# RWKV-6 and a SiLU layer on one core: the first two units loaded in runs of 16 tokens, and the way of their bonus sums

## Chip, core and metric

The kernel runs on one core of one Trainium2 chip. TensorE (PE, with weight loads PEld) multiplies matrices, VectorE (DVE), ScalarE (ACT) and GpSimd (POOL) work element by element, SyncE (SP) issues most DMAs; ACT issues some as well. Each engine does its instructions in order and waits on semaphores. The metric is the device time of one execution in microseconds (us).

## What is computed

The reference is a linear attention with decay and a bonus `u`, then two matrix products with SiLU between them:

```python
for t in range(S):                       # B, H, S, D = 4, 8, 768, 48
    cur = einsum('bhd,bhe->bhde', u[None] * k[t], v[t])
    y[t] = einsum('bhd,bhde->bhe', r[t], state + cur)
    state = w[t][:, :, :, None] * state + einsum('bhd,bhe->bhde', k[t], v[t])
x = y.transpose(0, 2, 1, 3).reshape(3072, 384)
h = x @ w_in                             # 384 x 2048
out = (h / (1 + exp(-h))) @ w_out        # 2048 x 384
```

The bonus of one token is the sum over d of r*u*k: it is the diagonal of the matrix of scores of a head. All is float32.

## The kernel before

The sequence is cut into 6 blocks of L = 128 tokens, the batch into 2 pairs; that gives 12 units of 128 tokens by NB = 2 batch rows by 8 heads. Within a unit the state is not stepped: queries and keys grow by the decay over 7 levels (NL) of blocks of 1, 2, 4 to 64 tokens, and at each level TensorE makes the scores between neighbouring blocks. The output of a unit then passes through both matrix products. The order of work is written out by hand (lines 1384 to 1463): every engine gets its instructions in the order of these calls, and while a unit's levels run, the matrix products of earlier units and the rounding of weights are put between them.

The change touches the first two units (i < NTOK = 2), which have a way of their own to load tokens.

- `load_tokens` (114) with `load_twos` (108) brings k, r and w of a unit to `raw`, two neighbouring tokens of one head in a run: 192 KB a DMA, one DMA for each batch row, a partition holding a pair of tokens of all 8 heads. For unit 0 the second batch row is issued by ACT, all else by SP.
- `turn_in` (370) turns such a tile on TensorE, channels to partitions, by matmuls with the identity as the moving operand, 128 columns each; `s` says whether the even or the odd tokens. `turn_out` (381) copies the PSUM bank to `tk`, `tr` or `tw` on ACT; for k the second batch row is written backwards.
- `bonus` (426) multiplies: step 0 r of odd by k of even tokens (needed for level 0), step 1 r by k, step 2 by `u_bc`, which holds u for all heads in each partition (line 281, 192 KB by a DMA broadcast). `bonus_sum` (446) adds over d on DVE into `own_sums`.
- `bonus_spread` (577) brings these sums to the layout of the scores, on TensorE with the matrix `spread` of zeros and ones that `make_spread` (302) builds; `bonus_write` (598), for unit 0 in four parts by `bonus_part` (606), puts them into `score` on DVE with a mask (line 602).
- `odd_ones` (658, ACT), `start_keys` (663), `grow_queries` (625), `product` (408) are level 0: they multiply keys (L670), queries (L628) and decays (L414). `odd_keys` (613, ACT), `grow_keys` (631, POOL, L646) and `scores` (725: TensorE L712 or L704, then `keep_masked` on DVE, L722) are the later levels.
- `beat` (1374) transposes the identity on TensorE, n times; the result is used by nobody.
- `head_weight` (ACT, 221), `tail_weight` (ACT, 232), `join_weight` (DVE, L247, L248) and `add_weight` (POOL, L260) round one piece of the weights; `up` (1079) is the first matrix product, `x_products` (883) the output of the attention. `tail_weight` writes to the PSUM tile `p_w`, in which unit 0's spread sums lie before it.

PSUM banks are given out in turn: `bank("p_m")` and `bank("p_sc")` alternate between two banks each. The first two units' steps are in this order (lines 1384 to 1387):

```python
do((make_spread,), (beat, 16), *both(turn, 0, "k"), (odd_ones, 0), (bonus, 0, 0), (bonus, 0, 1), *both(turn, 0, "r"),
   (bonus_sum, 0, 0), (clear_state,), (clear_rest,), *back(turn, 0, "w"), (bonus, 0, 2), (bonus_sum, 0, 1), (start_keys, 0, nc.vector, True),
```

then levels 1 to 6 of unit 0 (1393) with unit 1's turns between them, then unit 1 (1396 on). `kernel.py` in the profile has these line numbers.

## Time and profile before

| | us |
|---|---|
| median of 3 runs | 566.67 (566.48 to 567.2) |
| the profiled execution | 567.41 |
| its span | 565.6 |

| engine | busy us | share of the span |
|---|---|---|
| PE | 555.8 | 98% |
| DVE | 477.0 | 84% |
| POOL | 395.7 | 70% |
| ACT | 274.5 | 49% |

The granted clock of TensorE is 1.0 over the whole span, DMA moved 57.59 MB in 206485 packets. The span is counted from the first instruction. A timeline line gives start, duration, engine, source line, operation, what is written and read, shapes and count; in brackets stands how long the engine was idle before it and what ended that. A line of the chain gives start, duration and what worked. A "q" behind an engine is its sequencer, which waits and issues and does not compute. fp32 matmuls are recorded twice each, so 8 matmuls show as 16.

### The profile page before, as it was taken

The page shows a single profiled execution, that of the slowest core. Times are in us where ns is not written, and L with a number is a line of the kernel's source. Part 1 is how long each engine was busy: PE and PEld are TensorE (multiplying, and loading weights), DVE is VectorE, ACT ScalarE, POOL GpSimd, SP SyncE. Part 2 cuts the span into 40 slices and gives each one's busy share as a digit, 9 for nine tenths or more (in the row PEclk, how much of TensorE's full clock was granted, in tenths as well). Part 3 has the DMA queues.
Part 4 walks back from the last instruction along what each step waited for, and adds up shares of the span by engine and source line. Part 5 has one row for each costly group of instructions (what it writes and reads, how often), then busy time and mean ns, then how long its engine had stood idle before and what let it go on. Part 6 is the DMA issues. An engine that isn't in the chain of part 4 may idle for free.

```text
span 565.6 us, 18886 instructions
## 1 busy us (share of the span) xinstructions
PE 555.8 (98%) x7782; PEld 517.6 (92%) x7782; DVE 477.0 (84%) x744; ACT 274.5 (49%) x620; POOL 395.7 (70%) x447
## 2 busy tenths in 40 slices
PE   8989999999999999999999999999999999999997
PEld 8767786699889999999999999999999999999997
DVE  7979788998999989999889989989989989882250
ACT  5679696362371373373374274274274272371330
POOL 5998988617879998969796696696696696700000
PEclk9999999999999999999999999999999999999999
DMA  9956876345345365365565554555555462102000
GB/s 224 314 104 191 213 213 133 49 69 115 99 76 99 80 105 94 59 131 95 104 104 93 113 93 89 108 96 94 111 88 95 99 102 65 38 5 57 29 9 21
DMA packets 206485, 57.59 MB, mean 102 GB/s; under 512 B 186048, under 2 KB 198208, under 8 KB 206400
## 3 DMA queue, kind: packets, MB, share of 16 engines
q1 hardware_dynamic: 203712, 54.23, 46.9%
q10 hardware_dynamic: 2688, 2.16, 1.6%
q8 instruction: 61, 1.00, 0.8%
q14 instruction: 24, 0.20, 0.1%
HBM read 47.14 MB, written 9.18 MB: 100 GB/s over the span
## 4 chain that ended last, share of the span: by engine, by line
PE 78%; DVE 8%; POOL 7%; DMA 3%; issue 2%; ACT 1%; SPq 0%; POOLq 0%; DVEq 0%
PE p_o L1335 24%; PE p_o L1191 14%; PE p_h L1191 9%; PE p_h L1084 8%; PE p_h L1335 4%; PE p_m L1273 4%; PE p_sc L704 3%; PE p_m L868 2%; PE p_sc L1335 2%; POOL tk L646 2%; POOL w_in_sb L260 2%; PE p_m L847 1%; DVE tr L628 1%; PE p_m L704 1%; POOL tw L414 1%
## 5 line engine op out<-in xcount | busy, mean ns | idle before, releaser
L646 POOL TENSOR_TENSOR tk<-tk,tw 128x256 f32<-128x256 f32 x112 | 91.7, 839 | 7.6 <-DVE tw L414 3.4
L1335 PE MATMUL p_o<-own,temps 128*128 128x192 f32 x496 | 82.9, 326 | 0.0
L1335 PEld LDWEIGHTS p_o<-own,temps 128*128 128x128 f32 x496 | 80.8, 190 | 0.3 <-DVE temps L1306 0.2
L1191 PE MATMUL p_o<-xt,w_in_sb 128*64 128x128 f32 x1152 | 72.5, 273 | 0.1
L414 POOL TENSOR_TENSOR tw<-tw 128x256 f32<-128x256 f32 (+6 forms) x71 | 42.3, 596 | 38.0 <-DVE tw L365 34.5
L1084 PE MATMUL p_h<-xt,w_in_sb 128*128 128x256 f32 x288 | 66.1, 384 | 1.8 <-POOL w_in_sb L260 1.6
L1191 PEld LDWEIGHTS p_o<-xt,w_in_sb 128*64 128x64 f32 x1152 | 64.9, 137 | 0.4 <-issue 0.4
L1084 PEld LDWEIGHTS p_h<-xt,w_in_sb 128*128 128x128 f32 x288 | 53.6, 190 | 10.0 <-POOL w_in_sb L260 2.4
L497 POOL TENSOR_TENSOR ruk<-tokens_rk 128x384 f32<-128x384 f32 x48 | 53.6, 1137 | 8.1 <-DMA tokens_rk<-in_k_dram 8.1
L1335 PE MATMUL p_o<-w_out_sb,gt 128*128 128x192 f32 x308 | 54.5, 330 | 0.4 <-DVE ob L1343 0.3
L628 DVE TENSOR_TENSOR tr<-tr,tw 128x512 f32<-128x512 f32 x57 | 51.9, 911 | 1.0 <-PE p_m L704 0.4
L1335 PEld LDWEIGHTS p_o<-w_out_sb,gt 128*128 128x128 f32 x308 | 50.0, 190 | 1.5 <-DVE ob L1343 0.9
L655 POOL TENSOR_TENSOR tk<-tk,tw 128x256 f32<-128x256 f32 x32 | 25.1, 812 | 27.5 <-DVE tk L365 27.5
L1306 DVE TENSOR_TENSOR temps<-gt 128x512 f32<-128x512 f32 (+1 forms) x48 | 42.9, 931 | 0.0
L1340 ACT COPY partial<-p_o 128x192 f32<-128x192 f32 x31 | 9.9, 319 | 66.6 <-PE p_o L1335 61.5
L616 ACT COPY tk<-tk 128x256 f32<-128x256 f32 x52 | 20.9, 402 | 37.2 <-POOL tk L646 27.4
L1215 ACT ACTIVATE gt<-p_o 128x512 f32<-128x512 f32 x45 | 26.0, 601 | 25.0 <-PE p_o L1191 25.0
L1335 PE MATMUL p_o<-w_out_sb,temps 128*128 128x192 f32 x176 | 30.5, 326 | 0.0
L722 DVE COPY_PREDICATED score<-mask,p_sc 128x512 f32<-128x512 int8 x38 | 28.4, 807 | 1.4 <-PE p_sc L704 1.3
L1335 PE MATMUL p_h<-w_out_sb,gt 128*128 128x192 f32 x168 | 29.1, 326 | 0.0
L1335 PEld LDWEIGHTS p_o<-w_out_sb,temps 128*128 128x128 f32 x176 | 28.9, 190 | 0.1
L497 POOL TENSOR_TENSOR spare<-tokens_rk 128x384 f32<-128x384 f32 x24 | 28.5, 1198 | 0.6
(251 smaller groups left out, 1314.0 us busy)
## 6 DMA issues: line engine op xcount, KB each, us to landing
w_out_sb<-in_moe_w_in_dram SPq DMA_DIRECT2D x6, 768.0 KB, 7.4
turned<-yt SPq DMA_DIRECT2D x18, 192.0 KB, 2.7
xt<-turned SPq DMA_DIRECT2D x9, 384.0 KB, 3.3
w_out_sb<-in_moe_w_out_dram SPq DMA_DIRECT2D x4, 768.0 KB, 7.4
own<-in_moe_w_out_dram SPq DMA_DIRECT2D x4, 768.0 KB, 4.7
tokens_w<-in_w_dram SPq DMA_DIRECT2D x8, 384.0 KB, 4.5
tokens_rk<-in_r_dram SPq DMA_DIRECT2D x7, 384.0 KB, 4.4
tokens_rk<-in_k_dram SPq DMA_DIRECT2D x7, 384.0 KB, 5.8
```

Of the source, the lines that this page charges most:

```text
L414: engine.tensor_tensor(out=up, in0=t[:, :, 0::2], in1=t[:, :, 1::2], op=ALU.mult)
L497: mul = lambda out, one, two: nc.gpsimd.tensor_tensor(out=out, in0=one, in1=two, op=ALU.mult)
L628: nc.vector.tensor_tensor(out=odd, in0=odd, in1=tw[i][l][:, :, 0::2][:, :, :, None].to_broadcast([128, Q, L >> (l + 1), c]), op=ALU.mult)
L646: nc.gpsimd.tensor_tensor(out=out, in0=have, in1=odd_products(i, l, b, *blocks), op=ALU.mult)
L655: nc.gpsimd.tensor_tensor(out=have, in0=have, in1=odd_products(i, l, b, [2, NP * ni]), op=ALU.mult)
L704: nc.tensor.matmul(to, lhsT=tk[i][rows, X[l % 2] + p, x * 64:(x + 1) * 64], rhs=have, start=True, stop=True)
L722: nc.vector.copy_predicated(out=dst, mask=masks[l][:, :, None].to_broadcast([128, NB, NP, ni, c]), data=sc[e].rearrange("p (b q) (i c) -> ...
L1084: nc.tensor.matmul(p_h[:, a, :], lhsT=w_in_sb[:, c, f * 128:(f + 1) * 128], rhs=xt[i][:, c, :], start=(a == 0 and c == 0), stop=(a == 1 an ...
L1191: nc.tensor.matmul(p[h:h + PD, q, :], lhsT=left[:, f:f + PD], rhs=right, start=first and q == 0, stop=q == 3, skip_group_check=True)
L1215: nc.scalar.activation(out=g(f, t), in_=have, func=AF.Silu)
L1306: nc.vector.tensor_tensor(out=out, in0=one, in1=two, op=op)
L1335: nc.tensor.matmul(p, lhsT=left(f), rhs=right[:, f, :], start=which in (0, 1, 3) and f == 0, stop=f == FH - 1, skip_group_check=True)
```

## The change

For units 0 and 1 a partition now holds 16 consecutive tokens of one head (`RUN`), so a DMA has 64 rows of 3072 bytes. Turning takes 16 matmuls of 64 columns for half of the tokens of a run, where there were 8 of 128; the moving operand is the identity with a stride, or, for k, `select`, in which the second batch row is reversed (built on POOL). r of unit 0 is turned into the p_sc banks, w of unit 0 into the two p_h tiles. A partition belongs to one head, so u is loaded as one row of 48 for each partition (`u_rows`, two DMAs of 12 KB each, in a part of `raw` that `clear_rest(1)` clears later), and the broadcast u_bc for the later units is loaded behind the weights and values. All products of unit 0's bonus and its `odd_ones` are done by POOL. The sums are written to DRAM by a DMA and read back by two more in another order (`bonus_read`), by ACT for unit 0 and SP for unit 1; `bonus_spread` then needs two matmuls, with the identity and its mirror image. `spread` is gone, with its memset and four copies. Unit 0's four score writes, one ahead of level 1 and one each after levels 2, 3 and 4, come after levels 3, 4 and (two) 5; unit 1's sums move from its level 2 to before its first `up`. The diff, without its unchanged lines:

```diff
+    RUN = 2 * BLK
     def load_tokens(i):
+        n, b0 = units[i]
...
-            load_twos(twos(raw[:, i % NSLOT, WRK[name]])[0], src, i, [nc.sync, nc.scalar if i == 0 else nc.sync])
+            room = twos(raw[:, i % NSLOT, WRK[name]])[0].rearrange("p h s -> p (h s)")
+            for b in range(NB):
+                queue = nc.scalar if i == 0 and b else nc.sync
+                queue.dma_start(out=room[b * L // 2:(b + 1) * L // 2],
+                                in_=src[b0 + b, :, n * L:(n + 1) * L, :].rearrange("h (i s) d -> h i (s d)", s=RUN))
...
-    def load_u():
+    def load_u_rows(to):
...
-            nc.sync.dma_start(out=u_bc[b * H * rows:(b + 1) * H * rows, 0],
+            nc.sync.dma_start(out=to[b * H * rows:(b + 1) * H * rows],
...
-    nc.sync.dma_start(out=u_bc, in_=u.partition_broadcast(128))
+    def load_u():
+        load_u_rows(u_bc[:, 0])
+    u_rows = raw[:, 1, 0].rearrange("p b h d -> p (b h d)")[:, H * 2 * D + PD - D:H * 2 * D + PD]
+    load_u_rows(u_rows)
...
+    nc.sync.dma_start(out=u_bc, in_=u.partition_broadcast(128))
...
-    spread = room[:, 0:4 * L].rearrange("p (s b t) -> p s b t", s=2, b=NB)
+    select = room[:, 0:2 * PD].rearrange("p (e m) -> p e m", e=2)
...
-    def make_spread():
+    def make_select():
+        have = ident.rearrange("k (b p e i) -> k b e p i", b=NB, p=NP, e=2)
+        to = select.rearrange("k e (b p i) -> k b e p i", b=NB, p=NP)
+        for e in range(2):
+            nc.gpsimd.tensor_copy(out=to[:, 0, e], in_=have[:, 0, e])
+            nc.gpsimd.tensor_copy(out=to[:, 1, e], in_=have[:, 1, e, ::-1, ::-1])
+    def make_mirror():
...
-        for s in range(2):
-            nc.scalar.copy(out=spread[0:L // 2, s, 0, s::2], in_=ident[0:L // 2, 0:L // 2])
-            nc.scalar.copy(out=spread[L // 2:L, s, 1, L - 1 - s::-2], in_=ident[L // 2:L, L // 2:L])
...
-    nc.gpsimd.memset(spread, 0.0)
...
-    nc.gpsimd.memset(score, 0.0)
+    def clear_score():
+        nc.gpsimd.memset(score, 0.0)
...
-    def turn_in(i, s, name):
-        flat = raw[:, i % NSLOT, WRK[name]].rearrange("p b h d -> p (b h d)")
-        p_tr = bank("p_m", NP, NB, L // 2)
-        for p in range(NP):
+    def turn_rows(to, flat, places, back):
+        to = to[:] if not isinstance(to, bass.AP) else to
+        have = ident.rearrange("k (b p e i) -> k e b p i", b=NB, p=NP, e=2)
+        width = to.shape[1] // (NB * NP * (L // RUN))
+        step = NP * (L // RUN) * width
+        for n, (at, z, z1) in enumerate(places):
...
-                at = ((2 * p + e) * 2 + s) * D
-                nc.tensor.matmul(p_tr[PD * e:PD * e + PD, p].rearrange("p b i -> p (b i)"), lhsT=flat[:, at:at + PD],
-                                 rhs=ident, start=(p == 0), stop=(p == NP - 1))
-        turned[i, s, name] = p_tr
-    def turn_out(i, s, name, t):
-        p_tr = turned.pop((i, s, name))
+                rows = to[PD * e:PD * e + PD]
+                nc.tensor.matmul(bass.AP(tensor=rows.tensor, offset=rows.offset + z,
+                                         ap=[rows.ap[0], [step + z1 - z, NB], [(L // RUN) * width, NP], [width, L // RUN]]),
+                                 lhsT=flat[:, at:at + PD], rhs=select[:, e] if back else have[:, e], start=(n == 0),
+                                 stop=(n == len(places) - 1), skip_group_check=True)
+    def halves(x, back):
+        have = range(x * RUN // 2, (x + 1) * RUN // 2)
+        if back:
+            have = [s for s in range(RUN) if (RUN // 4 <= s < RUN - RUN // 4) == (x == 1)]
+        place = {s: z for z, s in enumerate(have)}
+        return [(s * D, place[s], place[RUN - 1 - s] if back else place[s]) for s in have]
+    def turn_in(i, x, name, flat=None):
+        if flat is None:
+            flat = raw[:, i % NSLOT, WRK[name]].rearrange("p b h d -> p (b h d)")
+        if (i, name) == (0, "w"):
+            p_tr = ps.tile([128, 512], F32, name="p_h", bufs=2)
+        else:
+            p_tr = bank("p_sc" if (i, name) == (0, "r") else "p_m", 512)
+        turn_rows(p_tr, flat, halves(x, name == "k"), name == "k")
+        turned[i, x, name] = p_tr
+    def turn_out(i, x, name, t):
+        p_tr = turned.pop((i, x, name))
+        copy = nc.scalar.copy
+        half = p_tr[:].rearrange("p (q i s) -> p q i s", q=Q, s=RUN // 2)
...
-            to = t[:, NP:].rearrange("p q (i s) -> p q i s", s=2)
-            nc.scalar.copy(out=to[:, 0:NP, :, s], in_=p_tr[:, :, 0])
-            nc.scalar.copy(out=to[:, NP:2 * NP, :, 1 - s], in_=p_tr[:, ::-1, 1, ::-1])
+            quarter = RUN // 4
+            to = t.rearrange("p q (i s) -> p q i s", s=RUN)[:, (NP if t.shape[1] > Q else 0):][:, 0:Q]
+            if x == 1:
+                copy(out=to[:, :, :, quarter:3 * quarter], in_=half)
+            else:
+                copy(out=to[:, :, :, 0:quarter], in_=half[:, :, :, 0:quarter])
+                copy(out=to[:, :, :, 3 * quarter:], in_=half[:, :, :, quarter:])
...
-            to = t.rearrange("p (b q) (i s) -> p q b i s", b=NB, s=2)[:, :, :, :, s]
-            nc.scalar.copy(out=to, in_=p_tr)
-    def clear_rest():
-        for i in range(NSLOT):
-            nc.gpsimd.memset(raw[:, i].rearrange("p x b h d -> p x (b h d)")[:, :, H * 2 * D + PD - D:], 0.0)
+            copy(out=t.rearrange("p q (i z s) -> p z q i s", z=2, s=RUN // 2)[:, x], in_=half)
+    def clear_rest(i):
+        nc.gpsimd.memset(raw[:, i].rearrange("p x b h d -> p x (b h d)")[:, :, H * 2 * D + PD - D:], 0.0)
...
+    pairs = own_sums.rearrange("p s h q -> p (s h q)").rearrange("p (a s q) -> p s a q", a=H, s=2)
+    def bonus_read(i):
+        kept, diag[i] = diag[i], pt.tile([128, NB, H, 2], F32, name="both_b", bufs=1)
+        for b in range(NB):
+            (nc.scalar if i == 0 else nc.sync).dma_start(
+                out=diag[i][:, b], in_=kept[b * L // 2:(b + 1) * L // 2].rearrange("(h i) (t q) -> (i t) h q", h=H, q=2))
     def bonus(i, x):
-        engine = nc.gpsimd if i > 0 or x == 0 else nc.vector
+        engine = nc.gpsimd if i > 0 else nc.vector
...
-            engine.tensor_tensor(out=ruk[i], in0=ruk[i], in1=u_bc[:, :, None, :].to_broadcast([128, H, 2, D]), op=ALU.mult)
+            engine.tensor_tensor(out=ruk[i], in0=ruk[i], in1=u_rows[:, None, None, :].to_broadcast([128, H, 2, D]) if i < NTOK else u_bc[:, :, None, :].to_broadcast([128, H, 2, D]),
+                                 op=ALU.mult)
     def bonus_sum(i, x):
+        sums = pairs if i < NTOK else own_sums
...
-            nc.vector.tensor_reduce(out=own_sums[:, 0, :, 1], in_=ruk[i, 0], axis=mybir.AxisListType.X, op=ALU.add)
+            nc.vector.tensor_reduce(out=sums[:, 0, :, 1], in_=ruk[i, 0], axis=mybir.AxisListType.X, op=ALU.add)
...
-            nc.vector.tensor_reduce(out=own_sums[:, s, :, s], in_=ruk[i][:, :, s], axis=mybir.AxisListType.X, op=ALU.add)
+            nc.vector.tensor_reduce(out=sums[:, s, :, s], in_=ruk[i][:, :, s], axis=mybir.AxisListType.X, op=ALU.add)
...
+            kept = diag[i] = scratch.tile([128, 4 * H], F32, name="pairs")
+            (nc.scalar if i == 0 else nc.sync).dma_start(out=kept, in_=own_sums.rearrange("p s h q -> p (s h q)"))
...
     def bonus_spread(i):
...
-            if i == 0:
-                diag[i] = p_w[:, 0, 0:NB * H * 2].rearrange("p (b h s) -> p b h s", b=NB, h=H)
-            else:
-                diag[i] = bank("p_m", NB, H, 2)
+            have, diag[i] = diag[i], (p_w[:, 0, 0:NB * H * 2] if i == 0 else bank("p_m", NB * H * 2)).rearrange("p (b h s) -> p b h s", b=NB, h=H)
...
-                for s in range(2):
-                    nc.tensor.matmul(diag[i][:, b].rearrange("p h s -> p (h s)"), lhsT=spread[:, s, b, :],
-                                     rhs=own_sums[:, s].rearrange("p h s -> p (h s)"), start=(b == 0 and s == 0),
-                                     stop=(b == NB - 1 and s == 1))
+                nc.tensor.matmul(diag[i][:, b].rearrange("p h s -> p (h s)"), lhsT=(ident, mirror)[b],
+                                 rhs=have[:, b].rearrange("p h s -> p (h s)"), start=True, stop=True)
...
     def odd_ones(i):
-        nc.scalar.copy(out=keys(i, X[1] * L + 1, [1, NB], [4, NP * L // 4], [1, 1]),
-                       in_=keys(i, NP * L + 1, [NP * L + 1, NB], [4, NP * L // 4], [1, 1]))
+        copy = nc.gpsimd.tensor_copy if i == 0 else nc.scalar.copy
+        copy(out=keys(i, X[1] * L + 1, [1, NB], [4, NP * L // 4], [1, 1]),
+             in_=keys(i, NP * L + 1, [NP * L + 1, NB], [4, NP * L // 4], [1, 1]))
...
-    do((make_spread,), (beat, 16), *both(turn, 0, "k"), (odd_ones, 0), (bonus, 0, 0), (bonus, 0, 1), *both(turn, 0, "r"),
-       (bonus_sum, 0, 0), (clear_state,), (clear_rest,), *back(turn, 0, "w"), (bonus, 0, 2), (bonus_sum, 0, 1), (start_keys, 0, nc.vector, True),
-       (start_keys, 0, nc.vector, False), (grow_queries, 0, 0), (product, 0, 0, nc.vector), (odd_keys, 0, 1), (grow_keys, 0, 1),
-       (beat, 3), (bonus_spread, 0), (beat, 5), (bonus_part, 0))
+    do((make_select,), (clear_score,), (beat, 16), *both(turn, 0, "k"), (odd_ones, 0), (bonus, 0, 0), (bonus, 0, 1), *both(turn, 0, "r"),
+       (bonus, 0, 2), (bonus_sum, 0, 0), (clear_state,), (clear_rest, 0), *both(turn, 0, "w"), (bonus_sum, 0, 1), (make_mirror,), (start_keys, 0, nc.vector, True),
+       (start_keys, 0, nc.vector, False), (grow_queries, 0, 0), (product, 0, 0, nc.vector), (grow_keys, 0, 1), (odd_keys, 0, 1), (bonus_read, 0),
+       (beat, 8))
...
-    others = {1: [(beat, 6)], 2: [(turn, 1, 0, "r"), (head_weight, 0), (beat, 2), (bonus_part, 1)],
-              3: [(turn, 1, 1, "r"), (head_weight, 1), (beat, 2), (bonus_part, 2)], 4: [(turn, 1, 1, "w"), (reverse_v, 0), (bonus_part, 3)],
-              5: [(turn, 1, 0, "w")], 6: [(turn_in, 1, 0, "k"), *blocks[0:4], (tail_weight, 0)]}
+    others = {1: [(beat, 6)], 2: [(turn, 1, 0, "r"), (head_weight, 0), (beat, 2)],
+              3: [(bonus_spread, 0), (turn, 1, 1, "r"), (head_weight, 1), (bonus_part, 0)], 4: [(turn, 1, 1, "w"), (reverse_v, 0), (bonus_part, 1)],
+              5: [(turn, 1, 0, "w"), (bonus_part, 2), (bonus_part, 3)], 6: [(turn_in, 1, 0, "k"), *blocks[0:4], (tail_weight, 0)]}
...
-    do((bonus, 1, 0), (bonus, 1, 1), (product, 1, 0), (bonus, 1, 2), *both(x_products, 0), (join_weight, 0), (add_weight,),
+    do((bonus, 1, 0), (bonus, 1, 1), (product, 1, 0), (bonus, 1, 2), (clear_rest, 1), *both(x_products, 0), (join_weight, 0), (add_weight,),
...
-       (odd_ones, 1), (add_weight,), (start_keys, 1, nc.gpsimd, True), (head_weight, 2), (grow_queries, 1, 0), (tail_weight, 2),
-       (up, 0, 0), (turn_k, 0), (join_weight, 2), *blocks[4:8],
+       (odd_ones, 1), (add_weight,), (start_keys, 1, nc.gpsimd, True), (head_weight, 2), (grow_queries, 1, 0), (bonus_sum, 1, 0), (bonus_sum, 1, 1), (tail_weight, 2),
+       (up, 0, 0), (turn_k, 0), (join_weight, 2), (bonus_read, 1), *blocks[4:8],
...
-    others = {1: [(bonus_sum, 1, 0), (bonus_sum, 1, 1), (load_rk, 2)], 2: [*both(update, 0), *blocks[8:10]],
+    others = {1: [(load_rk, 2)], 2: [*both(update, 0), *blocks[8:10]],
...
```

## The prediction

> **What bounds the kernel now.** I read the page first (PE 98% busy, chain 78% on PE), then busy time by stretch, to see where PE is not full.
>
> ```profile
> 0.00:14.00 14.00, 12.50 (x134) 11.39 (x136) 10.06 (x48) 7.49 (x17) 8.43 (x22) 1.00 0.97 224
> 28.00:45.00 17.00, 14.80 (x186) 11.83 (x182) 12.22 (x15) 13.24 (x23) 15.36 (x14) 1.00 0.64 150
> 63.00:110.00 47.00, 46.83 (x367) 33.95 (x359) 40.24 (x50) 27.86 (x44) 40.38 (x40) 1.00 0.62 139
> ```
>
> The columns are stretch, length, and busy time of PE, weight load, DVE, ACT, POOL, then clock, DMA share, GB/s. From 63 us on PE has 0.17 us idle in 47: nothing there can be shortened by this change, and whatever starts that stretch later ends the run later by as much. So the question is when it starts. The chain of waits says what leads to it:
>
> ```profile
> 1.36 3.67 PE p_m L1378 x16
> 5.03 2.78 PE p_m L377 x32
> ...
> 8.54 0.68 ACT tk L660
> ...
> 10.95 0.65 ACT tw L389
> ...
> 11.62 1.31 DVE tk L670 x4
> 12.93 0.60 DVE tr L628
> 13.53 0.61 DVE tw L414
> ...
> 14.27 1.89 POOL tk L646 x2
> ...
> 63.33 2.86 PE p_h L1084 x12
> ```
>
> No DMA stands in it ahead of 14 us: k's turn begins when the 16 beats end, w's when ACT has emptied a p_m bank. From 14.27 to 63.3 DVE and POOL take turns, with PE between them at 26 to 31, and no gap worth naming. A delay at L670, the first multiplication of the keys, is passed on.
>
> The DVE and POOL timelines show what else stands ahead of L670:
>
> ```profile
> 7.11 0.96 DVE L442 TENSOR_TENSOR tokens_rk<-raw 128x768 f32<-128x768 f32 x1 [1.56 <-DMA raw<-in_r_dram]
> 9.44 0.95 DVE L444 TENSOR_TENSOR tokens_rk<-tokens_rk,u_bc 128x768 f32<-128x768 f32 x1
> 10.42 1.01 DVE L453 TENSOR_REDUCE own_sums<-tokens_rk 128x8 f32<-128x384 f32 x2
> 11.62 1.31 DVE L670 TENSOR_TENSOR tk<-tk,tw 128x128 f32<-128x128 f32 x4 [0.18 <-ACT tw L389]
> 7.56 1.38 POOL L440 TENSOR_TENSOR tokens_rk<-raw 128x384 f32<-128x384 f32 x1
> 30.03 1.82 POOL L444 TENSOR_TENSOR tokens_rk<-tokens_rk,u_bc 128x768 f32<-128x768 f32 x1
> ```
>
> Today the bonus of unit 0 (products on DVE, sums by L453 to 11.43) ends just before w is there at 11.59, so it costs nothing.
>
> **The change, part by part.** Times below are of the profiled execution: 567.41 us, its span 565.6, so 1.81 around it. It lies 0.74 above the median 566.67; I add the difference to the median.
>
> *Loads in runs of 16.* 192 KB come as 64 rows of 3072 bytes instead of 512 of 384. On the chain: 0, since beats and banks, not data, time the turns. Off it, the early DMA (share 0.97 to 1.05 until 28 us) gets lighter; no engine waits for a weight there.
>
> *Turns.* Twice the matmuls of half the columns. Nearest row: L913 (128 rows by 48 columns, 48 moving) has 16 recorded in 0.45 us, so 64 columns take about 0.6 and a half turn of 32 recorded 1.1 to 1.2; today 16 recorded L377 take 1.09. Bounds -0.1 to +0.2 a half turn. Strided operands cost nothing: L712 takes 1.16 to 1.18 us with runs of 2 and of 32. With r in p_sc and w in p_h no bank is waited for: k ends at 7.8, w at about 11.6, ACT's second w copy (0.64) at 12.2. L670 now needs both halves of w, where today the odd one sufficed, so 12.25 instead of 11.62 if nothing else were late. k's copies: two of 0.29 pitch and one of 0.63 end at about 8.46, like today.
>
> *Bonus of unit 0.* This is the costly part. On POOL stand, in this order, the copy odd_ones, the products of bonus 0 and 1, and that with u; on DVE bonus_sum(0,1) now stands before start_keys and waits for all of them. odd_ones needs k's last copy: 8.50. Its cost on POOL has no row; 256 single elements, bounds 0.6 (128x256 product, L414) and 1.3 (two 128x128 products of single elements, L670 on POOL at 0.66); I take 0.7, as a copy reads one operand: 9.2. Product 0: 1.0 with DVE still (L440 later in the run), up to 1.4 as now: 10.2. Two of 128x768 at 1.82 and 1.81: 13.83. Two reductions 1.01 and two hand-overs 0.1: L670 at 14.9. That is **+3.3** (3.0 to 4.3). Queued behind that wait on DVE are start_keys, grow_queries(0,0), product(0,0); for them wait POOL's L646, idle from clear_rest on, and PE. ACT, whose queue holds the write to DRAM, also stands until 14.9, but its next work, odd_keys, needs start_keys.
>
> *Bonus written later.* Today's first L602 (0.74) ran while PE made the level 1 scores, at no cost. Now the four fall in levels 3 to 5, where DVE is full (13.63 of 14 us): one more at a pitch of 0.62: **+0.6**. tail_weight(0) waits for the last of them, but DVE's own level 6 ends later.
>
> *The way through DRAM.* Nothing of the kind in unit 0. The nearest rows are
>
> ```profile
> kept<-block_sums SPq DMA_DIRECT2D x8, 64.0 KB, 1.6
> spare<-kept SPq DMA_DIRECT2D x8, 32.0 KB, 4.7
> diag<-own_sums SPq DMA_DIRECT2D x8, 4.0 KB, 1.8
> ```
>
> 1.6 to 4.5 us out (4.5: the first four of L459, behind loads), 2.9 to 5.3 back in 1024 pieces. Written at 15.0, read from 16.8 at the earliest and 19.5 at the latest, both halves there by 20.1 to 25.2. PE asks for them in bonus_spread after the level 3 scores, at 19.96 + 3.3 - 0.4 = 22.9. So 0 to 2.3 late; I take **+0.9**, near the middle, for loads still fill the engines. Behind it on PE: turn(1,1,r) and the level 4 scores, for which DVE waits.
>
> *Unit 1.* clear_rest(1) on POOL (0.67) is covered by the wait of the second L260 for DVE (0.6 later anyway); without that cover +0.67. SP stands at bonus_read(1) until the write has landed, 2 to 4.5 us; behind it are block loads of unit 2 and weights whose tiles are worked on from about 70 us: 0. The sums of unit 1 leave the place in front of L247:
>
> ```profile
> 49.32 0.99 DVE L453 TENSOR_REDUCE own_sums<-tokens_rk 128x8 f32<-128x384 f32 x2
> 50.24 0.94 DVE L247 SCALAR_TENSOR_TENSOR p_w<-own,p_w 128x768 uint32<-128x768 uint32 x1
> 52.38 2.15 POOL L260 TENSOR_TENSOR w_in_sb<-temps 128x768 uint32<-128x768 uint32 x1 [1.15 <-DVE temps L248]
> ```
>
> They go into DVE's wait of 2.65 us before 37.16. L247 has its p_w from ACT at 49.45, so **-0.75** (at most -1.15, POOL's wait).
>
> Sum: 3.3 + 0.6 + 0.9 - 0.75 = **+4.05**; 566.67 + 4.05 = 570.7. Select copies, mirror, u rows (twice 12 KB) and the later u_bc lie in idle stretches: 0.
>
> **Rivals.**
>
> *PE slow after its pause.* PE now has nothing between the end of beat(8), 12.4, and the level 1 scores at 16.9: 4.5 us. Today's longest pause here is 1.5 us and leaves the pitch as it was. But the span begins slow: the beats come every 213 ns until 6.5 us, later every 109. If 4.5 us bring that back, level 1 scores take 2.3 instead of 1.16 (+1.15, straight on the chain) and level 2 up to 1.1 more, half of it under DVE: +1.2 to +2.2, so 572 to 573. Chance 0.18. The Trainium skill, "TensorE: Matmul & The Clock Gate", Part 1, says that a whole idle window of about 3.4 us halves PE's clock; by it alone this rival would hold whenever a window falls inside the pause. The granted clock of 1.00 in the profile's slices does not show the slow start, only the pitch does.
>
> *The read from DRAM is late.* PE stands at bonus_spread for the full 2.3 us or more, with ACT held at the read's issue too: another +1.4 to +2.5, 572.1 to 573.2. For it: DMA share above 1 until 28 us; against: lighter loads. Chance 0.13.
>
> *The slip is absorbed.* If POOL's products ended by 11.2, L670 would start at 12.25, +0.6, and the sum is 0.6 + 0.6 - 0.75 = +0.5: 567.2. That needs POOL to start at 5.9 (5.33 earlier), when k's turn isn't done. Chance 0.08.
>
> *Faster.* One mechanism: DVE, relieved of its sums in unit 1, stops holding up POOL's weight additions. POOL's waits for L248 between 33 and 57 us are 0.33 + 0.64 + 0.67 + 1.15 + 0.23 = 3.0; if all went and the slip were only 0.6 + 0.6, -1.8: 564.9. It decides from a slip under 1.3 at L670 (1.3 + 0.6 - 3.0 is 1.1 gained), that is L670 before 12.9. Only one of the five waits follows a moved sum. Chance 0.06. That the change doesn't do what it says (loads no lighter) changes nothing on the chain.
>
> **The numbers.** My forecast has 0.55, from 568.6 to 572. Both late mechanisms give up to 573.2, and odd_ones and product 0 at their upper bounds add 1.0; with the absorbed case at the low end the range is 567.2 to 574. A measurement tells 0.2%, 1.1 us, from no change: faster is below 565.5 (0.06), same up to 567.8 (0.08), slower 0.86.
>
> **What the profile will show.** Right: L670 on DVE near 14.9 with a wait for POOL's u product before the reductions; POOL from 8.5 to 13.9 without a gap; PE idle from about 12.4; level 3 followed by a short PE wait for DMA; PE full from about 67.4 instead of 63.3. Wrong: L670 at 12.3; or a DVE that catches up between 28 and 63; a pitch of 213 in level 1 is the clock rival, a PE wait over 2 us at bonus_spread the DRAM one.

## The result and the profile after

| | before | after |
|---|---|---|
| median, same chip, 4 runs each | 566.64 us | 584.18 us (582.44 to 588.54) |
| profiled execution, its span | 567.41, 565.6 | 584.81, 583.0 |
| mean granted clock of PE | 1.0 | 0.98 |

The ratio is 1.0319, 95% interval [1.0262, 1.0377]: 17.5 us slower, where 4 were forecast and 574.0 was the upper end of the range. (Ratios leave out executions over 1.5% above the kernel's fastest: two of four with the beats alone, the profiled one among them, and one of four, also the profiled one, with the trip first, whose trip is therefore read from the trace of the kernel with more beats.)

One statement on record is wrong in itself. The section on the change says that POOL does all products of unit 0's bonus, and the prediction costs them there. The changed code has `engine = nc.gpsimd if i > 0 else nc.vector`: for unit 0 they are on **DVE**. Only `odd_ones` went to POOL.

Busy time by stretch, after (columns as in the prediction):

```profile
0.00:14.00 14.00, 9.91 (x211) 9.37 (x212) 7.38 (x43) 4.74 (x9) 7.24 (x24) 1.00 0.56 158
14.00:28.00 14.00, 9.97 (x97) 8.27 (x95) 7.94 (x15) 3.77 (x8) 5.67 (x10) 0.64 0.92 225
28.00:45.00 17.00, 12.98 (x209) 10.89 (x210) 10.27 (x14) 7.50 (x16) 11.41 (x14) 0.69 0.72 189
63.00:110.00 47.00, 46.47 (x447) 36.93 (x448) 39.69 (x51) 38.03 (x56) 42.60 (x44) 1.00 0.73 179
```

DMA is used less in the first 14 us (share 0.56, 158 GB/s; before 0.97, 224), every engine has less work until 45, and PE's clock is 0.64 and 0.69 where it was 1.00. The record of the granted clock has 0.50 from 17.9 to 38.4 us and once more from 55.5 to 58.9; all four executions have a mean clock of 0.980 to 0.984. PE is full from 79.2 instead of 63.3: of the 17.4 us by which the span grew, 15.9 are lost by then.

The chain of waits, after (start, us, what):

```profile
3.56 8.45 DMA raw<-in_u_dram
...
12.13 0.96 DVE tokens_rk L496
13.09 0.47 DVE own_sums L503
13.55 0.92 DVE own_sums L507 x2
14.47 1.18 DVE tk L722 x4
15.65 0.59 DVE tr L679
16.24 6.47 DMA pairs<-own_sums
...
22.74 0.38 ACTq L475
...
23.16 6.95 DMA both_b<-pairs
...
30.14 0.61 PE p_w L638 x2
30.75 1.91 PE p_m L396 x32
...
42.10 1.37 DVE score L653 x2
```

Before, no DMA stood in the chain up to 63 us. Now three do: the rows of u, the write of the sums to DRAM and their read. The rows of u land at 12.0; the keys' multiplication (L722, formerly L670) starts at 14.39 by the timeline; the sums take 6.47 us to DRAM and 6.95 back (13.9 with the issue between them; these two legs are called the trip below), then PE goes on at 30.14. At the end of unit 0 two score writes stand in a row.

The trip also began late. The sums were done at 14.47 and ACT's copies ahead of the write at 14.33, but the write was issued only at 16.24. Until then ACT's sequencer waited for the semaphore that the write was to use: an earlier DMA on it, k of unit 1, landed at 16.16.

What the slip is made of can be read by laying the same instruction of DVE in both traces side by side. A masking is a `keep_masked` of one level (L722 before, L774 after), a join is L247 or L255. The start of the keys alone lies between 11.18 and 11.79 in variants of the kernel before that do the same work up to there, so a few tenths in one trace mean nothing.

| starts at (us) | before | after | slip | what came in since the row above |
|---|---|---|---|---|
| keys' first multiplication | 11.62 | 14.39 | +2.77 | loads, u rows, both halves of w |
| last masking of level 2 | 19.17 | 22.81 | +3.64 | half clock |
| last masking of level 3 | 21.61 | 29.07 | +7.46 | ACT stands at the read's issue |
| last masking of level 4 | 24.34 | 36.01 | +11.67 | PE waits for the read; half clock |
| masking of level 5 | 26.34 | 41.34 | +15.00 | half clock; DVE held by a product of POOL |
| masking of level 6 | 27.34 | 43.56 | +16.22 | two score writes in front of it |
| sixth join of the weights | 50.24 | 66.07 | +15.83 | sums of unit 1 moved away (fifth join: +16.59) |

Three lines of other engines' timelines show how the trip reaches the levels. They are of ACT, POOL and PE:

```profile
22.74 1.01 ACTq L475 DMA_DIRECT2D both_b<-pairs  x2
23.79 0.41 ACT L667 COPY tk<-tk 128x256 f32<-128x256 f32 x1 [4.42 <-PE p_m L396]
24.34 1.29 POOL L697 TENSOR_TENSOR tk<-tk,tw 128x256 f32<-128x256 f32 x2 [4.86 <-ACT tk L667]
30.14 0.61 PE L638 MATMUL p_w<-both_b,partial 128*128 128x16 f32 x2 [1.85 <-DMA both_b<-pairs]
```

ACT must wait for the write before it can issue the read; behind that stands its copy of the keys (`odd_keys`, L667), for which POOL stands 4.86 us and with it level 3. The profile puts the copy's 4.42 us down to PE, the semaphore that came last before it; but with the read moved away (below) the same copy follows the one ahead of it within 0.4 us. What held it is the read's issue, which stood until 22.74.

One more row of the table needs its lines, of DVE and POOL:

```profile
39.52 1.90 DVE L679 TENSOR_TENSOR tr<-tr,tw 128x512 f32<-128x512 f32 x1 [2.19 <-PE p_h L764]
39.05 1.82 POOL L494 TENSOR_TENSOR tokens_rk<-raw 128x768 f32<-128x768 f32 x1
```

The multiplication of the queries at level 5 took 1.90 us, where 0.69 to 0.71 is usual; it stands in the chain. It began while POOL was at a product of unit 1's bonus (to 40.87) and ended 0.55 us behind it (41.42). So 1.2 of the 3.33 us between levels 4 and 5 are not PE's clock itself. In the kernel without the trip, where PE had its clock by then, the same multiplication took 0.69; whether the half clock brought the two together here is likely, but not shown.

### The profile page after: what moved, and what is told of

It is laid out like the page before. It is cut to its first block, busy times and chain, and to the rows that moved or that the text cites. A ratio compares the mean times of both kernels' runs of the same rounds, so it can differ in the third digit from the quotient of the medians.

```text
span 583.0 us, 19258 instructions
## 1 busy us (share of the span) xinstructions
PE 562.9 (97%) x7964; PEld 523.8 (90%) x7964; DVE 477.4 (82%) x745; ACT 272.5 (47%) x613; POOL 395.7 (68%) x450
## 4 chain that ended last, share of the span: by engine, by line
PE 81%; DVE 6%; DMA 5%; POOL 4%; SPq 2%; issue 2%; ACT 0%; ACTq 0%; DVEq 0%; POOLq 0%
PE p_o L1387 26%; PE p_o L1243 15%; PE p_h L1243 10%; PE p_h L1136 8%; PE p_h L1387 4%; PE p_m L1325 4%; PE p_sc L756 3%; PE p_m L920 2%; PE p_sc L1387 2%; POOL w_in_sb L268 2%; PE p_m L899 2%; PE p_m L756 1%; DMA raw<-in_u_dram 1%; POOL tk L697 1%; DMA both_b<-pairs 1%
## 5 line engine op out<-in xcount | busy, mean ns | idle before, releaser
L1136 PE MATMUL p_h<-xt,w_in_sb 128*128 128x256 f32 x288 | 67.8, 391 | 0.5 <-POOL w_in_sb L268 0.5
L667 ACT COPY tk<-tk 128x256 f32<-128x256 f32 x52 | 20.9, 402 | 41.4 <-POOL tk L697 27.3
L774 DVE COPY_PREDICATED score<-mask,p_sc 128x512 f32<-128x512 int8 x38 | 28.4, 805 | 1.4 <-PE p_sc L756 1.3
```

What stands on the lines that cost most here:

```text
L774: nc.vector.copy_predicated(out=dst, mask=masks[l][:, :, None].to_broadcast([128, NB, NP, ni, c]), data=sc[e].rearrange("p (b q) (i c) -> ...
L1136: nc.tensor.matmul(p_h[:, a, :], lhsT=w_in_sb[:, c, f * 128:(f + 1) * 128], rhs=xt[i][:, c, :], start=(a == 0 and c == 0), stop=(a == 1 an ...
```

## The experiments

Before and after are the kernels of the table; a kernel that "leaves out the bonus" has no sums of units 0 and 1 in the scores. Each ratio is to the kernel before on the same chip (medians 567.0 to 567.4).

**Loads and trip, each alone and together.** The loads of one tensor as one DMA whose slowest dimension is 16 rows (batch and head) instead of two with 8 (head):

```diff
-            for b in range(NB):
-                queue = nc.scalar if i == 0 and b else nc.sync
...
+            queue = nc.scalar if i == 0 and name == "r" else nc.sync
+            queue.dma_start(out=room, in_=src[b0:b0 + NB, :, n * L:(n + 1) * L, :].rearrange("b h (i s) d -> (b h) i (s d)", s=RUN))
```

> The changed kernel, but k, r and w of a unit come by one DMA of both batch rows each (384 KB, still rows of 3072 bytes), so that the outermost count of the source is 16 and not 8. Theory A: the loads of the change are late because a DMA whose outermost count is 8 is spread over 8 of the 16 engines only (each of ACT's three loads ends with 8 packets of 4 bytes instead of 16); then r and w of unit 0 land 2 to 4 us sooner, the first key product (14.39 in the changed kernel) begins at 11.6 to 12.6, the way through DRAM, with less queued ahead of it, takes 8 to 12 us instead of 13.9, and the run takes 575 to 581 us. Rival B: the loads are late because of their long rows or because of what is queued, whatever the number of engines; then the landings move by less than 0.7 us and the run stays at 582 to 588.

Measured 584.22, ratio 1.0293 [1.0272, 1.0315]. Of theory A only the landings came; the keys, the trip and the total were missed. r lands at 7.4 instead of 9.2 and w at 8.75 instead of 11.6, but k at 7.15 instead of 5.8, a window of half clock (8.4 to 11.8) met the turns, and the keys start at 15.31, later than with 8 rows. SP then ran further ahead with weights, and write to landed read took 17.8 us instead of 13.9.

Without the trip (both DMAs gone, the tile cleared by POOL; leaves out the bonus):

```diff
-            (nc.scalar if i == 0 else nc.sync).dma_start(out=kept, in_=own_sums.rearrange("p s h q -> p (s h q)"))
...
+        nc.gpsimd.memset(diag[i], 0.0)
```

> The changed kernel without the way through DRAM: the sums of units 0 and 1 are neither written nor read, the bonus that goes into the scores is zero (POOL clears its tile), so the bonus of these two units is left out of the result; all else is done. Theory A: ACT's stand until 22.7 us and PE's until 30.1 come from the DMAs alone, and the half clock between 17.9 and 38.4 follows from these pauses. Without them PE is full from 66 to 69 us instead of 79.2, and the run takes 570 to 574 us. Rival C: it is the clock that falls by itself, because of the pause at 14.7 to 16.4 and the lighter matmuls of 64 columns; then the clock still falls at about 18 us and the run takes 574 to 580.

Measured 573.55, ratio 1.0106 [1.009, 1.0121]: theory A's time. Against the kernel before on each chip the change cost 17.5 us and this kernel 6.4, so the trip with all that follows from it is about 11 us. Rival C is there too, but smaller: with no DMA to wait for, the clock in the trace still fell for two windows (16.7 to 23.5).

Both edits together (leaves out the bonus):

> Both edits together: loads over 16 engines, and no way through DRAM (bonus of units 0 and 1 left out as before). Theory A: nothing of the change is left that costs but the turn's wait for both halves of w (0.6) and the score writes in full levels (0.6), less the 0.75 of the moved sums: 566 to 569 us. Rival D: the 64-column turns, odd_ones on POOL or the later score writes cost by themselves: 570 or more.

Measured 570.91 (569.89 to 574.49), ratio 1.0085 [1.0053, 1.0116], clock 1.0 throughout in the trace: rival D. The median is 2.6 us below that of the kernel with 8 rows, but the two intervals overlap. Surer is the trace: the keys start at 12.94 instead of 14.11, 1.2 us earlier, and the executions at clock 1.0 differ by as much (571.88 with 8 rows, 570.70 and 570.91 with 16). 3.8 us to the kernel before are left that neither edit explains.

**The read later.** The read after level 3, spread and writes after level 6:

```diff
+              3: [(turn, 1, 1, "r"), (head_weight, 1), (bonus_read, 0)], 4: [(turn, 1, 1, "w"), (reverse_v, 0)],
+              5: [(turn, 1, 0, "w")], 6: [(turn_in, 1, 0, "k"), (bonus_spread, 0), *[(bonus_part, x) for x in range(4)], *blocks[0:4], (tail_weight, 0)]}
```

> The changed kernel with everything computed, but unit 0's read from DRAM issued after level 3 and its spread and four score writes after level 6, so that neither ACT at level 1 nor PE at level 3 stands for a DMA. Theory A: the two waits go (about 4.9 us of POOL behind ACT, 1.9 of PE, and what the clock makes of them); the four writes come back as 2.5 us at the end of unit 0, and the read may land after level 6 (issue at 21 to 23, 7 us to landing): 573 to 579 us. Rival C (the clock falls by itself): 578 to 584.

Measured 582.73, ratio 1.0268 [1.0251, 1.0285]. ACT no longer stands in level 3 (last masking of level 3 at 25.24, slip 3.63 instead of 7.46), so that term is +3.8. Theory A's time was missed all the same: the second read was issued only at 30.04, and PE waited in another place:

```profile
37.17 0.54 PE L638 MATMUL p_w<-both_b,ident 128*128 128x16 f32 x2 [2.87 <-DMA both_b<-pairs]
39.22 0.61 PE L638 MATMUL p_w<-both_b,partial 128*128 128x16 f32 x2 [1.51 <-DMA both_b<-pairs]
```

The clock stayed at 1.0 until 37.3, so rival C's mechanism did not come; it fell behind the window in which PE stood for the read. Moving the reader does not help while the transfer itself is late.

**Why the trip is slow: the queue ahead of it, or its small pieces.** Loads as above, and the trip of unit 0 on SP ahead of the weights and values:

```diff
-    load_weight(1)
-    load_values(0)
...
+    def load_rest():
+        load_weight(1)
+        load_values(0)
...
-            (nc.scalar if i == 0 else nc.sync).dma_start(out=kept, in_=own_sums.rearrange("p s h q -> p (s h q)"))
+            nc.sync.dma_start(out=kept, in_=own_sums.rearrange("p s h q -> p (s h q)"))
...
+       ... (odd_keys, 0, 1), (bonus_read, 0), (load_rest,),
```

> The changed kernel, everything computed, with one load for both batch rows (16 rows as the slowest dimension) and with the write and the read of unit 0's bonus sums issued on SP ahead of the weights and values, which now wait until the read is issued. Theory A (the way through DRAM is slow because its small packets and its semaphores stand behind the loads already queued): write and read together take at most 7 us instead of 13.9 (after) and 17.8 (16-engine loads alone), PE has its clock throughout, and the run takes 571 (569.5 to 573), the time that the kernel without the trip had with such loads (570.9). Rival B (the pieces of 8 bytes are slow by themselves, whatever is queued): the read alone still takes 6 us or more, PE stands for it again, 578 to 584. Rival C (the weights and values come too late now): PE waits for a weight tile in the levels, with the trip itself short.

Measured 573.76, ratio 1.0102 [1.0074, 1.0131], everything computed: over 10 us of the change's loss are back, and A's window was missed by 0.8. The same trip is seen in the trace of the next kernel, which adds beats to it:

```diff
-    do((make_select,), (clear_score,), (beat, 16), ...
+    do((make_select,), (clear_score,), (beat, 26), ...
...
-       (beat, 8))
+       (beat, 16))
```

> The kernel with 16-engine loads and the way through DRAM ahead of the weights (573.8, everything computed), with more idle multiplications: 26 instead of 16 until the tokens land, 16 instead of 8 ahead of the level 1 scores. Theory A (what this kernel still has over the 570.9 of the one without the trip is half clock at the start and after the pause; its timed runs had a mean clock of 0.993 to 0.997): clock 1.0 (0.997 at least) throughout, 570 to 572, and less spread between its runs. Rival B (the trip still holds PE up, or the weights put back come late): 573 to 575 at clock 1.0. Rival C (beats at the slow pitch push k's turn back): 573 to 575 with k's turn starting after 7 us.

SP and then PE of this kernel:

```profile
11.23 0.34 SPq L510 DMA_DIRECT2D pairs<-own_sums  x1
16.05 2.03 SPq L475 DMA_DIRECT2D both_b<-pairs  x2
18.13 0.57 SPq L217 DMA_DIRECT2D w_out_sb<-in_moe_w_in_dram  x1
```

```profile
22.85 0.40 PE L638 MATMUL p_w<-both_b,ident 128*128 128x16 f32 x2
23.09 0.38 PE L638 MATMUL p_w<-both_b,partial 128*128 128x16 f32 x2
```

The write took 4.8 us (unit 1's tokens were still ahead of it), and the 2048 pieces of 8 bytes ran from 17.1 to 19.5; in the changed kernel they ran from 23.9 to 29.4. PE no longer waits (no bracket). So the pieces by themselves need 2.4 us, and rival B is out: theory A, with 8.3 instead of 7 us for the trip. The edit moved the trip ahead of the weights and from ACT's queue to SP's at once; which of the two did it is not separated. Time: 574.86, ratio 1.0129 [1.0103, 1.0155], not better than without the beats; even the execution at clock 1.0 missed the 570 to 572 of theory A. Its four executions are 572.7 with a mean clock of 1.0, 573.7 with 0.994 and 576.1 twice with 0.987: the clock is not held in all of them.

**The clock.** Only more beats in the changed kernel:

```diff
-        (beat, 8))
+        (beat, 22))
...
-     others = {1: [(beat, 6)], 2: [(turn, 1, 0, "r"), (head_weight, 0), (beat, 2)],
-               3: [(bonus_spread, 0), ...
+     others = {1: [(beat, 12)], 2: [(turn, 1, 0, "r"), (head_weight, 0), (beat, 30)],
+               3: [(beat, 24), (bonus_spread, 0), ...
```

> The changed kernel with more idle multiplications of TensorE (beats): 22 instead of 8 after the turns, 12 instead of 6 after level 1, 30 instead of 2 after level 2 and 24 new ones ahead of the wait for the bonus; nothing else changed, the way through DRAM too. Theory A (the half clock comes from the half-idle window at 14.5 to 17.9 us, and costs by itself some 6 of the 17 us): the granted clock stays at 1.0 until 60 us, the levels have the pitch of before, and the run takes 576 to 580. Rival B (the clock is lost anyway, since PE stands for the read): half clock from 24 or 28 us on, 581 to 585. Rival C (the beats, in order on PE, push the scores back by more than the clock gives): over 584 at clock 1.0.

Measured 578.1 to 587.6, median 585.72, ratio 1.0239 [1.0185, 1.0293]: no clear gain. Only the fastest execution, with a mean clock of 0.996, lies in theory A's range. The trace, of an execution of 587.27, shows the mechanism. The clock stayed at 1.0 until 32.4 instead of 17.9 us, and level 2 slipped no further than the keys (both +3.32; in the changed kernel the slip grew by 0.87 there). Then PE stood 3.37 us for the read, which landed at 33.8 this time, and the clock went to 0.50 until 42.7: rival B's mechanism. Beats in the queue hold the clock only up to an instruction that waits.

The same question in the kernel before, where nothing is late: without its 18 beats in unit 0's levels.

```diff
-       (beat, 3), (bonus_spread, 0), (beat, 5), (bonus_part, 0))
+       (bonus_spread, 0), (bonus_part, 0))
...
-    others = {1: [(beat, 6)], 2: [(turn, 1, 0, "r"), (head_weight, 0), (beat, 2), (bonus_part, 1)],
+    others = {1: [], 2: [(turn, 1, 0, "r"), (head_weight, 0), (bonus_part, 1)],
...
```

> The kernel before without the 18 idle multiplications of unit 0 after the turns (3 and 5 around the spread, 6 after level 1, 2 after levels 2 and 3); the 16 at the start stay. No pause of TensorE gets longer than about 2 us, but from 11.7 to 24 us it is busy about half of the time. Theory A (a window of 3.4 us that is about half busy is enough to halve the clock, and the half clock costs by itself): windows at 0.50 between 14 and 30 us, the levels stretched, 569 to 572. Rival B (only a pause of a whole window halves it, and in the changed kernel it was the late data): clock 1.0 and 567, as before. Rival C (half clock, but hidden behind DVE and POOL): windows at 0.50 and 567 to 568.

Measured 568.02, ratio 1.002 [1.0004, 1.0036], +1.0. Windows of this kernel, cut where the clock record changes (columns as above):

```profile
10.32:13.73 3.41, 2.63 (x38) 2.36 (x34) 2.62 (x8) 1.90 (x4) 0.13 (x1) 1.00 1.29 228
13.73:17.14 3.41, 1.96 (x29) 1.76 (x31) 3.38 (x5) 0.41 (x1) 2.63 (x4) 1.00 1.14 280
17.14:20.55 3.41, 3.41 (x32) 2.85 (x30) 3.41 (x5) 1.24 (x3) 3.33 (x6) 0.50 0.98 208
20.55:23.96 3.41, 3.41 (x57) 3.00 (x55) 2.70 (x6) 3.34 (x6) 2.44 (x5) 1.00 1.00 354
```

and the second of them in the kernel before:

```profile
13.73:17.14 3.41, 2.77 (x38) 2.40 (x38) 3.38 (x5) 0.41 (x1) 2.79 (x4) 1.00 1.14 274
```

With PE busy 2.77 of 3.41 us the clock stays; with 1.96, its longest pause 1.45, the next window runs at 0.50, and the slip of the maskings grows from 0.15 at level 2 to 0.93 at level 3. So theory A has the mechanism: a half-busy window can be enough, and one costs about 0.8 us in these levels. Its time of 569 to 572 was too high for the median, which is at rival C's upper end; only the two executions with a mean clock of 0.988 took that long (570.30, 570.88).

**The bonus on POOL, as I had read it.** In the kernel with 16-row loads and no trip (leaves out the bonus):

```diff
-        engine = nc.gpsimd if i > 0 else nc.vector
+        engine = nc.gpsimd
```

> The kernel with 16-engine loads and without the way through DRAM (it leaves out the bonus of units 0 and 1; 570.9), with unit 0's products of the bonus on POOL instead of DVE: that is what my sum of 3.3 us was worked out for. Theory A (that arithmetic was right for POOL): the first multiplication of the keys starts at 14.9 to 15.5 instead of 12.94, and the run takes 2 to 2.6 more, 572.9 to 573.5. Rival B (POOL works beside DVE and the sums end no later): the same 570.9. Rival C (PE's pause is now long enough for half the clock): 575 or more with a granted clock of 0.50 in the windows after 17 us.

Measured 575.28, ratio 1.0131 [1.01, 1.0162]. POOL of this kernel:

```profile
11.04 0.66 POOL L706 COPY tk<-tk 128x256 f32<-128x256 f32 x1 [3.75 <-ACT tk L426]
11.66 1.00 POOL L488 TENSOR_TENSOR tokens_rk<-raw 128x384 f32<-128x384 f32 x1
12.63 1.82 POOL L490 TENSOR_TENSOR tokens_rk<-raw 128x768 f32<-128x768 f32 x1
14.53 1.81 POOL L492 TENSOR_TENSOR tokens_rk<-tokens_rk,raw 128x768 f32<-128x768 f32 x1
```

From the copy's start to the keys (17.30) are 6.26 us; my sum had 6.4. The arithmetic was right, for another program. The keys are still later than theory A's 15.5: the copy itself began 1.8 later than with DVE (9.24), and the record of the clock at 1.0 begins only at 10.3 us here, at 4.3 there. Around PE's pause of 4.16 us the clock was 0.50, from 17.2 to 27.4: rival C, in the time too.

**Where the score writes stand.** The kernel before with its four writes after levels 3, 4, 5 and 5:

```diff
-              5: [(turn, 1, 0, "w")], 6: ...
+              5: [(turn, 1, 0, "w"), (bonus_part, 2), (bonus_part, 3)], 6: ...
```

> The kernel before, with only the places of the four score writes changed: after the scores of levels 3, 4, 5 and 5 instead of after spread and levels 2, 3 and 4; everything else as before. My prediction's step: +0.6 (one more write beside a full DVE), 567.2. Theory A, from the chain of the two kernels measured: the two writes after level 5 (0.69 each) stand straight in front of level 6's masking on DVE, on the path: +1.2 to +1.4, 567.9. Rival B (DVE has slack there, the path runs through POOL): 0, 566.6.

Measured 568.32, ratio 1.0028 [1.0011, 1.0045], +1.3: theory A. DVE of this kernel:

```profile
25.76 0.73 DVE L722 COPY_PREDICATED score<-late_masks,p_h 128x512 f32<-128x512 int8 x1
26.52 1.37 DVE L602 COPY_PREDICATED score<-own_mask,p_w 128x512 f32<-128x512 int8 x2
28.00 0.73 DVE L722 COPY_PREDICATED score<-late_masks,p_sc 128x512 f32<-128x512 int8 x1
```

In the kernel before a wait of 0.27 for PE stood in place of the 1.37. The other way round, the 16-row kernel without the trip (leaves out the bonus) with spread and writes back at their old places:

```diff
-       (beat, 8))
+       (beat, 3), (bonus_spread, 0), (beat, 5), (bonus_part, 0))
...
+    others = {1: [(beat, 6)], 2: [..., (beat, 2), (bonus_part, 1)],
+              3: [..., (bonus_part, 2)], 4: [..., (bonus_part, 3)],
```

> The kernel with 16-engine loads and without the way through DRAM (leaves out the bonus of units 0 and 1; 570.9), with the spread and the four score writes back at the places of the kernel before (spread ahead of level 1, writes after spread and levels 2, 3, 4). What remains of the change is the loads, the half turns, the products and the moved sums. Theory A (late writes and spread cost 1.1 to 1.5 of the 3.8 that remain, keys 1.3 later and half turns the rest): 569.3 to 570, and masking of the last level some 2.5 later than in the kernel before instead of 3.9. Rival B (the levels are held by PE's half turns of unit 1 whatever the writes do): 570.5 to 571.

(The clearing of the sums' tile on POOL also moves, ahead of w's turn.) Measured 571.12, ratio 1.0073 [1.0056, 1.009], above both theories' ranges; three of its four executions have a clock of 0.994 (570.7 to 572.2), and so the medians of this kernel and of the one with late writes (570.91) do not tell. Their profiled executions, both at clock 1.0, are 569.22 and 570.91. In these the masking of level 6 is 1.69 and 3.90 later than before, with the keys 1.49 and 1.32 later: half turns cost 0.2 in the levels, and with late spread and writes 2.4 more are lost (3.90 - 1.32 = 2.58, less 0.2). Of these 2.4, some 0.7 are there at level 1 already, ahead of any late write (0.5 of them a multiplication of DVE that took 1.20 us beside a product of POOL), so the late writes cost 1.7 to 2.4. What the two writes ahead of level 6's masking add is nearly the same wherever they stand there: 1.22 to 1.24 in eight of nine traces (1.53 in the other).

**The moved sums alone, in the kernel before.**

```diff
-       ... (grow_queries, 1, 0), (tail_weight, 2),
+       ... (grow_queries, 1, 0), (bonus_sum, 1, 0), (bonus_sum, 1, 1), (tail_weight, 2),
...
-    others = {1: [(bonus_sum, 1, 0), (bonus_sum, 1, 1), (load_rk, 2)], ...
+    others = {1: [(load_rk, 2)], ...
```

> The kernel before with only the three sums of unit 1's bonus moved to the place that the change gives them, ahead of the join of the second block, where DVE waits for ACT. My prediction's step: -0.75, 566.2 against 567.0. Rival (POOL and ACT take over the chain there): 0. The trace should show the sixth join of the weights 0.75 earlier.

Measured 566.75, ratio 0.9993 [0.9984, 1.0002]: the time does not tell it from nothing, nor from -0.75. Its trace has one window of half clock at 38.9, behind which the fifth join is 0.29 later than before; the sixth is 0.47 earlier, so 0.76 came in between the two.

With r and w of unit 0 turned in p_sc and p_h besides:

```diff
-        p_tr = bank("p_m", NP, NB, L // 2)
+        if (i, name) == (0, "w"):
+            p_tr = ps.tile([128, NP, NB, L // 2], F32, name="p_h", bufs=2)
+        else:
+            p_tr = bank("p_sc" if (i, name) == (0, "r") else "p_m", NP, NB, L // 2)
```

> The kernel before with unit 1's sums moved as above, and with unit 0's r and w turned in banks of their own (p_sc and p_h) as in the change, instead of waiting for ACT to empty the p_m banks. -0.75 for the sums; the first multiplication of the keys now waits for the bonus sums on DVE (to 11.43) instead of w (11.59): another 0 to -0.2. 566.0 (565.8 to 566.3), faster than both kernels. Rival: with w early the sums on DVE set the start and nothing more is gained than by the sums alone, 566.2; or the sums gain nothing, 566.8 to 567.

Measured **566.37, ratio 0.9983 [0.9974, 0.9991]**: faster than both kernels, than the one before by 1.0 us. DVE of this kernel:

```profile
34.31 0.55 DVE L452 TENSOR_REDUCE own_sums<-tokens_rk 128x8 f32<-128x384 f32 x1
34.78 1.00 DVE L456 TENSOR_REDUCE own_sums<-tokens_rk 128x8 f32<-128x384 f32 x2
37.04 0.96 DVE L247 SCALAR_TENSOR_TENSOR p_w<-w_out_sb,p_w 128x768 uint32<-128x768 uint32 x1 [1.26 <-ACT p_w L236]
...
49.38 0.96 DVE L247 SCALAR_TENSOR_TENSOR p_w<-own,p_w 128x768 uint32<-128x768 uint32 x1 [0.52 <-ACT p_w L236]
```

The sums lie in a wait that was 2.65 us long, 1.26 of it is left, and the sixth join comes at 49.38 instead of 50.24. Of these 0.86 the sums gave 0.75, between the fifth join and the sixth. The other 0.11 were there at the keys (11.51); as these started at 11.47 in the kernel with only the sums moved, a gain by the banks is not shown. The forecast and its first rival are not told apart.

**The mended change with the clock held.** The kernel with the trip first and 26 and 16 beats, and more of them in the levels:

```diff
-    others = {1: [(beat, 6)], 2: [(turn, 1, 0, "r"), (head_weight, 0), (beat, 2)],
-              3: [(bonus_spread, 0), (turn, 1, 1, "r"), ...
+    others = {1: [(beat, 12)], 2: [(turn, 1, 0, "r"), (head_weight, 0), (beat, 8)],
+              3: [(bonus_spread, 0), (turn, 1, 1, "r"), (beat, 8), ...
```

> The kernel with 16-engine loads, the way through DRAM ahead of the weights and 26 and 16 idle multiplications (574.9 in four runs of which the one with clock 1.0 throughout took 572.7), with 12 instead of 6 after level 1, 8 instead of 2 after level 2 and 8 new ones after level 3. Theory A (the rest of its spread is the clock): clock 0.997 to 1.0 in all runs and 572 to 573. Rival B (beats push scores back in order): 573.5 to 575 at clock 1.0. Rival C (the clock is lost at the start, by where its windows fall, whatever these beats do): runs at 0.987 to 0.994 again, 573.5 to 576.

Measured 573.13, ratio 1.0112 [1.0084, 1.014]. Three executions with a clock of 0.997 to 1.0 took 572.4 to 573.3; the profiled one, 576.09, lost two windows at 16.4 to 23.2 behind a window in which PE was busy 1.3 of 3.41 us. Theory A for three executions, rival C for one. That it depends on where the windows fall is likely, but with one trace for each kernel it is not shown. What is left of the change at full clock is 5.3 to 6.3 us (572.4 to 573.3 less 567.0).

## Why the prediction was wrong, point by point

The direction was right, the size wrong by a factor of four. In the order of its steps:

- *Loads, "on the chain: 0, since beats and banks, not data, time the turns"*: **failed**, +2.8 at the keys. k landed at 5.8 and its turn waited for it (1.2 us of PE), r and w at 9.2 and 11.6, the rows of u at 12.0. Each of ACT's three loads left 8 packets of 4 bytes behind, the completion marks, where those of before had left 16: half of the DMA engines did the work. The Trainium skill, "DMA: Bandwidth & Descriptors", section "Why a DMA increments its semaphore by 16 and not by 1", says that the number of engines is the largest number up to 16 that divides the slowest dimension of both sides; with 8 heads as the slowest dimension that is 8. The 8 marks agree. Without the trip, 16 rows brought the keys forward by 1.2 us; with it, in one trace, by nothing. I had looked at packet sizes and not at the shape of the pattern. Of +2.77, 1.3 to 1.5 stay with 16 rows: I had +0.63 for waiting for both halves of w, but k then still lands at 6.3, after the beats.
- *Turns*: right. A half turn takes 1.15 at full clock, and half turns cost the levels 0.2.
- *Bonus on POOL, +3.3*: **failed**, from misreading the diff. The products stayed on DVE, and the keys slipped by 2.77 for another reason. That the two numbers are close is chance.
- *Score writes, +0.6*: too small. 1.1 in the trace and 1.3 in the time when moved alone; two of them stand straight ahead of level 6's masking (1.22 to 1.24). With the late spread it is 1.7 to 2.4.
- *The way through DRAM, +0.9, at most 2.3*: **failed, and the largest miss**. The bounds of 4.5 and 5.3 us came from rows of a later stage and were not bounds: 6.47 and 6.95, up to 12.2 for the read in the kernel with faster loads. The write was issued 1.8 us after the sums were done, behind another load on its semaphore. And I had followed ACT's wait for the sums, not the one at the read's issue: `odd_keys` of the next level was queued behind it. That alone is +3.8. PE's wait for the read gives about 2.2 more, and the half clock under it about 2.0 (see the clock below). "Lighter loads" I had counted in the trip's favour; in the kernel with 16 rows they let SP run ahead, and the trip grew to 17.8 us. The sign that I had set, a wait of PE over 2 us at `bonus_spread`, stayed just under its bound at 1.85: ACT's stand had put level 3 back, so PE asked at 27.7 instead of 22.9.
- *Moved sums, -0.75*: right in the traces, 0.75 (with the banks) and 0.77 (without the trip).
- *The rival of the clock, 0.18, +1.2 to +2.2*: came, by another mechanism and larger. I priced one pause of 4.5 us and two levels; PE's longest pause ahead of 17.9 was 1.7 us, in a window busy for 1.73 of 3.41 us, and the half clock lasted six windows. It is 0.87 in level 2. In level 4 it is about 2.0, an estimate: spread, turn and scores of PE took 0.61, 1.98 and 2.08 us, and 0.38, 1.15 and 1.16 where the clock was 1.0. Of the 3.33 between levels 4 and 5, 0.44 are lost at full clock too, 1.2 are DVE's multiplication behind POOL, and 1.7 are left for the clock. That is 4.6 in all. The pause of 1.5 us by which I had judged that a short pause does nothing (36.6 to 38.1 before) lay across two windows, which kept PE busy for 2.56 and 2.69 us. The Trainium skill, "TensorE: Matmul & The Clock Gate", Part 1, gives the length of the window right, 3413 ns and running freely, but names an idle window as the condition. Here no window was idle: half-busy ones were enough.
- *The rival "the read is late", 0.13*: it named ACT's stand, at +1.4 to +2.5 in all; it was +3.8, and 2.2 for PE's wait.

Two things stay open. Behind the sixth join the changed kernel loses another 1.6 us, nearly all of it idle time of PE: 0.9 is one wait for DVE at 287.9, 0.4 lie at the end, and why they come was not traced. The mended kernels lose 0.2 to 1.5 there. And the clock's fall at 17.9 is not fully explained: windows as busy as the one ahead of it kept the clock in other kernels.

## What to carry to other kernels

Before a DMA's pattern is changed, look at its slowest dimension as well as at its packets, and at who is queued behind the instruction that waits to issue it: a round trip through DRAM put on a compute engine's queue stops that engine until the first leg has landed. The price of such a trip is set by the loads issued before it, so it is read from the stage in which it will run, or the trip is issued ahead of them. Where work on PE is taken out of a stretch in which it is near half busy, count the busy time of each 3.4 us beside the longest pause, and expect executions of one kernel to differ.

## What the runs showed of the hardware

- PE's granted clock changed only at the ends of windows of 3.41 us. In fifteen traces it fell to 0.50 behind all ten windows in which PE was busy 1.42 us or less, behind six of the fourteen with 1.68 to 1.95, and behind none with 2.0 and more. No pause within one of these windows was longer than 2.9 us. The longest pause does not separate them better: 1.45 to 2.87 where it fell, up to 1.73 where it stayed. The same kernel gave 572.7 with a mean clock of 1.0 and 576.1 with 0.987.
- From 0.50 the clock came back behind one window in which PE was busy throughout (17.1 to 20.6 in the kernel before without its beats), or behind two (31.6 to 38.4 in the changed kernel).
- A multiplication of DVE (128x512) that began during one of POOL ended 0.55 us behind POOL's: at 41.42 behind 40.87 in the changed kernel, at 17.56 behind 17.01 in the one with 16 rows and no trip. It took 1.90 and 1.20 us instead of 0.69.
- In these programs SP's and ACT's DMAs share eight semaphores in turn, and a DMA is issued only when the earlier one on its semaphore has landed. So the write waited until 16.24 for k of unit 1 (landed 16.16). With the read moved later its second half was issued at 30.04, when a weight of 768 KB on the same semaphore had landed (30.02), although nothing else held it.
